# A maximum read ahead of the fifth gate of six, and a last output block emptied token by token

## The chip, the cores and the metric

The kernel runs on one core of one Trainium2 chip. The metric is the time of one launch on the device in microseconds (us), as the median of several runs. Five engines work side by side, each on its own queue of instructions in a fixed order: TensorE (PE, matmuls; PEld is its weight loads), VectorE (DVE), ScalarE (ACT), GpSimd (POOL) and SyncE (SP, which here only issues DMA transfers). They wait for each other by semaphores.

## The reference

Two stages, one behind the other: a convolution-like attention over the last seven positions with softmaxed weights, and a feed-forward layer with a sigmoid gate on its result.

```python
w = weight_gen - np.max(weight_gen, axis=-1, keepdims=True)     # weight_gen: (4, 4096, 8 heads, 7)
w = np.exp(w)
w = w / (np.sum(w, axis=-1, keepdims=True) + 1e-09)
x_pad = np.concatenate([np.zeros((B, pad, D), dtype=np.float32), x], axis=1)   # x: (4, 4096, 192)
x_unf = x_pad[:, idx, :].reshape(B, S, K, H, group)             # the 7 positions up to each one
x = np.einsum('bshk,bskhg->bshg', w, x_unf).reshape(B * S, D)   # 16384 tokens x 192
...
h = x @ w_in                                                    # 192 -> 2048
g = h * (1.0 / (1.0 + np.exp(-1.702 * h)))
return (g @ w_out).astype(np.float32)                           # 2048 -> 192
```

## The kernel before, in words

The 16384 tokens are cut into 32 **blocks** of 512 (4 tokens on each of 128 partitions), and the 2048 hidden features into 16 slices of 128. A **unit** is one slice for one block, 512 in all. Each unit goes through these steps:

- `whole` (L391 to L394): four matmuls of 512 columns write h into a PSUM bank, and `halves` (L403, L404) adds the small rest. The numbers are split into f16 parts so that the sums keep f32 quality.
- `gate`: ACT takes a tanh of the bank (L409, tile `th`), DVE multiplies it into the bank (L410).
- `split`: ACT writes the f16 high part (L415), DVE the low part (L416), both into the tile `g`.
- `second` (L426 to L428): twelve matmuls of 192 columns a unit add its share to the output banks `o`, two tokens to a bank.

Units are worked in **groups** of six (after a first short group of two), since six PSUM banks `h0` to `h5` hold h. Within a group PE runs three units' `whole`, all `halves`, and then, for the units 0 to 5 in turn, the seconds of the group before, mixed with the remaining three `whole`. `gate(u)` of a unit comes ahead of `split` of the unit before it in the order of DVE and ACT.

Beside this runs the preparation of later blocks, in **steps** that a table of numbers places: `plan([n - 7.4, ...], gen)` runs one step of a generator where the unit count reaches that number, and `until(end)` runs all steps that are due. `n` is the first unit of the group in which a block begins, so `n - 12` to `n - 6` is the group before the last one ahead of it. One generator, `scales(blk)`, finds the power of two by which a block is scaled. Its steps: DVE reduces the block to one value per partition (L234, L202, L207, tile `tf`); a one-column matmul on PE (L210) adds these up over the partitions into a PSUM bank (tile `top`); DVE reads it (**L216**); and three tiny DVE operations make the scale of it (`power`, L220 to L222). The bank that `top` borrows is `h2`, which the first unit of the next group needs: that unit's first matmul L391 may not start before L216 has read the bank. For block 1 it is an output bank `o` instead, which the next L426 needs.

The scaled block is then split (L275 on ACT, L278 on DVE, tile `xs`), turned by a DMA transpose (L284, tile `xt`), and half of it is copied by another DMA (L288, tile `xd`). L391 to L394 and L403 read `xt`, L404 reads `xd`.

At the start DVE and ACT also turn the raw weights into f16 parts (`parts_out`: L358 and L378 on ACT, L360 on DVE). `store` empties an output bank: ACT copies two tokens (L435) and SP stores the block (L440); the last block is stored in two halves.

Of the kernel before, what the change touches and what calls it, by code (L numbers as in the profile page):

```python
# [22 lines left out]
def conv_attention_then_ffn(  # L23
# [16 lines left out]
    J = 4  # L40
# [112 lines left out]
    def attend(blk):  # L153

        i, jb = divmod(blk, XB)
        w = wb[i][:, jb * J * H : (jb + 1) * J * H, :]
        xa[blk] = acc = apool.tile([P, J, D], F32, tag="acc", name="acc")
        for k in range(K):
            if k == 0:
                tap(blk, nc.gpsimd, acc, k, w)  # L160
            else:
                t = apool.tile([P, J, D], F32, tag="prod", name="prod", bufs=1)
                tap(blk, nc.gpsimd, t, k, w)
                nc.gpsimd.tensor_tensor(acc, acc, t, ALU.add)  # L164
            yield
# [261 lines left out]
        nc.tensor.matmul(o, lhsT=hi, rhs=wol[:, d], start=False, stop=False, skip_group_check=True)  # L427
        nc.tensor.matmul(o, lhsT=hi, rhs=woh[:, d], start=False, stop=z, skip_group_check=True)  # L428

    def store(blk, i, each=False):  # L430

        if i == 0:
            osb[blk] = opool.tile([P, J, D], F32, tag="osb", name="osb")
        j = slice(2 * i, 2 * i + 2)
        nc.scalar.activation(osb[blk][:, j, :], po.pop((blk, i)), AF.Copy, scale=scale[blk][:, 5:6])  # L435
        if i or each:
            j0 = 2 * i if each else 0
            b, t0 = blk // NJ, (blk % NJ) * J
            rows = out[b * S : (b + 1) * S, :].rearrange("(p t) d -> p t d", t=T)
            nc.sync.dma_start(rows[:, t0 + j0 : t0 + 2 * i + 2, :], osb[blk][:, j0 : 2 * i + 2, :])  # L440


    units = [(blk, f) for blk in range(NB) for f in range(NF)]
# [8 lines left out]
    def plan(slots, gen):  # L452
        for n in slots:
            todo.setdefault(math.floor(n), []).append((n, len(todo), gen))

    def once(fn, *args):
        fn(*args)
        yield
# [12 lines left out]
    def hold(t):  # L471

        nc.gpsimd.tensor_copy(held, t)

    with tc.manual_schedule():
        load_w(0)
        load_x(0, 0, J)
        load_tail(0)
        load_in(0)
        load_in(1)  # L480
        load_x(0, J, XB * J)
        load_in(2)
        load_tail(1)
        load_in(3)
        for c in range(4):
            load_out(c)
        load_w(1)
        load_x(1, 0, XB * J)
        constants()


        w_first = ps_h.tile([P, N], F32, tag="h0", name="w")[:, 0 : J * H * K].rearrange("p (n k) -> p n k", k=K)
        plan((-36.1, -35.7, -35.1, -34.6, -33.6), softmax(0, V, w_first))
        plan((-35.3, -34.7, -33.9, -33.2, -32.0), softmax(1, G_))
        plan((-36.2,), once(warm, 7, ident, P))
        plan((-32.1, -30.4, -27.7, -25.0), attend_first(w_first))
        plan((-24.9, -24, -23, -22, -21, -0.04, -0.03), attend(1))
        plan((-20.5, -18.3, -17.1, -17.1), scales(0))
        plan((-15.7, -13.6), split_first())
        raw = {"t": raw_t, "i": raw_i, "o": [raw_o[:, c * QC : (c + 1) * QC] for c in range(NO)]}  # L500
        for k, c, at, *slots in (
            ("t", 0, 0, -28.6, -23.2, -21.6),
            ("i", 0, 1, -27.4, -21.8, -19.7),
            ("i", 1, 2, -26.2, -18.4, -16.9),
            ("i", 2, 3, -24.6, -16.3, -14.5),
            ("t", 1, 4, -22.3, -14.9, -13.2),
            ("i", 3, 5, -20.4, -12.1, -10.1),
            ("o", 0, 6, -18.5, -10.7, -8.9),
            ("o", 1, 7, -13.9, -9.4, -7.5),
            ("o", 2, 8, -12.0, -7.2, -5.7),  # L510
            ("o", 3, 9, -10.8, -4.8, -0.6),
            ("o", 4, 10, -8.2, -0.05, 1.4),
            ("o", 5, 11, -6.3, 1.45, 1.9),
        ):
            plan(slots, narrow((k, c), raw[k][c], at))
        plan((-8.0, -7.1, -5.8), bound_in())
        plan((-5.0,), scales_gate(0))
        plan((-4.5, -3.5), parts_tail(0))
        plan((-3.8, -2.8), parts_in(0))
        plan((-0.05,), once(hold, w0l[:, DFF - 8 :]))  # L520
        plan((-2.75,), once(warm, 5, w0h, QC))
        plan((-3.2, -2.1), parts_in(1))
        plan((-2.5, -1.4), parts_tail(1))
        plan((-1.9, -0.7), parts_in(2))
        plan((-1.2, -0.06), parts_in(3))
        plan((1.95, 4.6, 4.65), bound_out())
        for c, slots in enumerate(((4.7, 5.2), (5.3, 5.8), (6.2, 6.7), (7.55, 7.9), (7.95, 8.1), (8.2, 8.6))):
            plan(slots, parts_out(c))
        plan((4.66,), scales_out(0))
        plan((7.7, 9.4, 9.45, 9.46), scales(1))  # L530
        plan((9.47,), scales_gate(1))
        plan((9.48,), scales_out(1))
        plan((9.49, 10.6), split_x(1))
        plan((10.65, 12), turn(1))

        for blk in range(2, NB):
            n = first(blk * NF)
            plan([n - 12.2, n - 7.4, n - 7.39, n - 7.38], scales(blk))
            plan([n - 6.28], scales_gate(blk))
            plan([n - 6.26], scales_out(blk))  # L540
            plan([n - 6.3, n - 6.2], split_x(blk))
            plan([n - 6.15, n - 5], turn(blk))
            if blk == 2:
                plan((-0.04, 0.5, 4.9, 6.4, 7.2, 7.25), softmax(blk, G_))
                plan((8.61,), once(lambda: hold(wos[:, NF * D - 8 :])))
                plan([8.62 + k for k in range(K)], attend(blk))
            elif blk == 3:
                plan((5.9, 7.26, 8.7, 10.7, 13.7, 17.6), softmax(blk, G_))
                plan([18 + 2 * k for k in range(K)], attend(blk))
            else:  # L550
                plan([n - 48.2, n - 48.1, n - 42.1, n - 36.15, n - 30.2, n - 30.1], softmax(blk, G_))
                plan([n - 30 + 2.2 * k for k in range(K)], attend(blk))
            if blk % XB == 0 and blk > XB:
                plan([blk * NF - 56.5], load_pair(blk // XB))

        def seconds(six):


            for z in zip(six[::2], six[1::2]):
                blk, f = z[0]  # L560
                for i in range(2):
                    if f in (0, NF - 2):
                        for j in (2 * i, 2 * i + 1):
                            for u in z:
                                second(u, j)
                        if f:
                            store(blk, i, each=blk == NB - 1)
                    else:
                        for j in range(J):
                            second(z[i], j)  # L570
                    yield

        sixes = [units[:few]] + [units[n : n + Q] for n in range(few, len(units), Q)]
        for k, us in enumerate([None] + sixes, -1):
            n, z = (min(todo), 0) if k < 0 else (units.index(us[0]), units.index(us[-1]) + 1)
            steps = sorted((t for i in range(n, z) for t in todo.get(i, ())), key=lambda t: t[:2])

            def until(end):
                while steps and steps[0][0] < end:
                    next(steps.pop(0)[2], None)  # L580

            if k < 0:
                until(z)
                continue
            due = seconds(sixes[k - 1] if k > 2 else sixes[0] + sixes[1] if k == 2 else ())
            early, late = us[:3], us[3:]
            if len(us) < Q:
                early, late = us, []
            for i, u in enumerate(early):
                bank(u)  # L590
                whole(u, True, False)
                if i == 1 or i == 0 and k > 2:
                    next(due, None)
                    until(n + 0.5 + 0.5 * i)
            for u in late:
                bank(u)
            for u, v in zip(us[::2], us[1::2]):
                halves(u, v, u in early, v in early)
            last = None
            for i, u in enumerate(us):  # L600
                if i > 1:
                    next(due, None)
                if u in late:
                    whole(u, False, True)
                gate(u)
                until(n + 0.5 + i)
                if last:
                    split(last)
                last = u
                until(min(n + 1 + i, z - 0.4))  # L610
            split(last)
            until(z)
            for _ in due:
                pass
        for _ in seconds(sixes[-1]):
            pass
# [29 lines left out]
```

## Time and profile before

| what | value |
|---|---|
| median of 3 runs | 1102.25 us (1102.07 to 1102.97) |
| the profiled execution's own time | 1101.69 us |
| its span, first to last instruction | 1099.7 us |
| mean granted clock of TensorE | 0.984 of full speed |
| busy: PE, DVE, ACT, POOL | 1050.0, 886.6, 703.6, 721.2 us |

The profile shows one execution. Its own time is 1.99 us longer than its span, which is what lies around the first and the last instruction; it is 0.56 us below the median of the three runs. An engine's busy time counts the whole of each matmul, though neighbours overlap; so PE's pace is read from the starts of its matmuls, not from their durations.

### The profile page before, as it was taken

Reading aid. Unit: us, or ns where it says so; the run is one execution under the profiler, and the core shown is the slowest. Engines: PE = TensorE matmul, PEld = TensorE weight load, DVE = VectorE, ACT = ScalarE, POOL = GpSimd, SP = SyncE. Lnnn points to the kernel's source line nnn. Section 1 sums busy time; section 2 is a strip of 40 time slices with the busy share of each in tenths; the row PEclk is TensorE's granted clock in tenths of the full one; section 3 lists DMA queues with packets and bytes.
Section 4 is the critical chain, followed back from the end, with each engine's and each line's share of the span. In section 5 each row is a group of like instructions: output and inputs, shape, how many; then the busy total and the mean of one; then the engine's idle time right before and its main releaser. Section 6 shows DMA issues by size and latency. Waiting matters only on the chain.

```text
span 1099.7 us, 22223 instructions
## 1 busy us (share of the span) xinstructions
PE 1050.0 (95%) x8821; PEld 732.6 (67%) x8821; DVE 886.6 (81%) x1556; ACT 703.6 (64%) x1251; POOL 721.2 (66%) x484
## 2 busy tenths in 40 slices
PE   4579999999999999999999999999999999999998
PEld 3146766676667676667766667666666766676666
DVE  8887877888797888879787877887887788788765
ACT  5765666666666666666666666656666666567655
POOL 4469758686855868685587768558775856786100
PEclk9689999999999999999999999999999999999999
DMA  9300120312012121301212120131212102101010
GB/s 305 119 17 16 39 83 18 91 32 91 15 32 77 32 91 32 87 18 32 76 33 90 32 80 27 32 77 32 88 35 74 33 17 91 33 21 44 15 30 18
DMA packets 73231, 60.71 MB, mean 55 GB/s; under 512 B 60588, under 2 KB 65964, under 8 KB 71592
## 3 DMA queue, kind: packets, MB, share of 16 engines
q1 hardware_dynamic: 73128, 59.30, 18.7%
q8 instruction: 69, 1.13, 0.4%
q14 instruction: 34, 0.28, 0.1%
HBM read 31.96 MB, written 12.58 MB: 41 GB/s over the span
## 4 chain that ended last, share of the span: by engine, by line
PE 83%; DVE 8%; ACT 6%; issue 2%; DMA 0%; ACTq 0%
PE o L426 14%; PE o L427 14%; PE o L428 14%; PE h L391 9%; PE h L392 9%; PE h L394 9%; PE h L393 9%; PE h L403 5%; DVE h L410 4%; ACT th L409 3%; DVE g L416 3%; ACT osb L435 1%; DVE tap L149 0%; ACT abs L337 0%; ACT g L415 0%
## 5 line engine op out<-in xcount | busy, mean ns | idle before, releaser
L426 PE MATMUL o<-wos,g 128*128 128x192 f16 x2048 | 505.7, 247 | 3.2 <-DVE s L216 3.2
L427 PE MATMUL o<-wol,g 128*128 128x192 f16 x2048 | 504.9, 247 | 0.5 <-DVE wol L360 0.5
L428 PE MATMUL o<-woh,g 128*128 128x192 f16 x2048 | 504.8, 246 | 0.0
L410 DVE SCALAR_TENSOR_TENSOR h<-th,h 128x512 f32<-128x512 f32 x512 | 347.0, 693 | 181.7 <-ACT th L409 174.6
L409 ACT ACTIVATE th<-h,s 128x512 f32<-128x512 f32 x512 | 342.4, 686 | 231.8 <-PE h L404 135.8
L416 DVE SCALAR_TENSOR_TENSOR g<-g,h 128x512 f16<-128x512 f16 x512 | 349.2, 682 | 13.7 <-ACT g L415 2.0
L164 POOL TENSOR_TENSOR acc<-acc,prod 128x768 f32<-128x768 f32 x186 | 346.3, 1862 | 14.6
L415 ACT ACTIVATE g<-h 128x512 f16<-128x512 f32 x512 | 305.0, 596 | 44.1 <-DVE h L410 44.1
L149 POOL TENSOR_TENSOR prod<-xb,wb 128x768 f32<-128x768 f32 x186 | 288.9, 1553 | 11.1
L426 PEld LDWEIGHTS <-g 128*128 128x128 f16 x2048 | 200.4, 98 | 75.7 <-issue 35.9
L427 PEld LDWEIGHTS <-g 128*128 128x128 f16 x2048 | 200.6, 98 | 39.5 <-issue 3.2
L391 PE MATMUL h<-xt,w0l 128*128 128x512 f16 x512 | 195.1, 381 | 10.4 <-DVE s L216 10.4
L428 PEld LDWEIGHTS <-g 128*128 128x128 f16 x2048 | 200.7, 98 | 0.8 <-issue 0.7
L394 PE MATMUL h<-xt,wth 128*128 128x512 f16 x512 | 195.1, 381 | 0.0
L393 PE MATMUL h<-xt,w0h 128*128 128x512 f16 x512 | 195.1, 381 | 0.0
L392 PE MATMUL h<-xt,w0h 128*128 128x512 f16 x512 | 195.1, 381 | 0.0
L143 POOL TENSOR_TENSOR wb<-wb,wr 128x224 f32<-128x224 f32 x31 | 17.9, 576 | 229.1 <-DVE wr L140 225.6
L278 DVE SCALAR_TENSOR_TENSOR xs<-acc,s,xs 128x512 f16<-128x512 f32 (+1 forms) x62 | 102.3, 1689 | 0.0
L394 PEld LDWEIGHTS <-wth 128*128 128x128 f16 x512 | 50.3, 98 | 61.1 <-issue 1.1
L393 PEld LDWEIGHTS <-w0h 128*128 128x128 f16 x512 | 50.2, 98 | 61.1 <-issue 1.1
L403 PE MATMUL h<-xt,tl 64*128 64x512 f16 x256 | 70.6, 381 | 2.4 <-DVE g L416 2.4
L404 PE MATMUL h<-xd,tl 64*128 64x512 f16 x256 | 70.7, 381 | 2.0 <-DVE g L416 2.0
(92 smaller groups left out, 523.2 us busy)
## 6 DMA issues: line engine op xcount, KB each, us to landing
xb<-in_x_dram SPq DMA_DIRECT2D x12, 1344.0 KB, 6.4
out_dram<-osb SPq DMA_DIRECT2D x31, 384.0 KB, 2.4
wb<-in_weight_gen_dram SPq DMA_DIRECT2D x16, 224.0 KB, 3.2
ro<-in_moe_w_out_dram SPq DMA_DIRECT2D x4, 768.0 KB, 12.3
xb<-in_x_dram SPq DMA_DIRECT2D x3, 768.0 KB, 7.4
ri<-in_moe_w_in_dram SPq DMA_DIRECT2D x4, 512.0 KB, 8.6
xb<-in_x_dram SPq DMA_DIRECT2D x4, 504.0 KB, 5.2
xd<-xt SPq DMA_DIRECT2D x31, 64.0 KB, 2.1
```

The lines of the kernel that those rows point to most:

```text
L164: nc.gpsimd.tensor_tensor(acc, acc, t, ALU.add)
L391: nc.tensor.matmul(ps, lhsT=w0l[:, s], rhs=x0, start=start, stop=False)
L392: nc.tensor.matmul(ps, lhsT=w0h[:, s], rhs=x2, start=False, stop=False)
L393: nc.tensor.matmul(ps, lhsT=w0h[:, s], rhs=x0, start=False, stop=False)
L394: nc.tensor.matmul(ps, lhsT=th_[:, s], rhs=x1, start=False, stop=stop)
L409: nc.scalar.activation(t, hp[u], AF.Tanh, scale=scale[u[0]][:, 4:5])
L410: nc.vector.scalar_tensor_tensor(hp[u], t, 1.0, hp[u], ALU.add, ALU.mult)
L415: nc.scalar.activation(g[:, 0], hp[u], AF.Copy, scale=2.0**-12)
L416: nc.vector.scalar_tensor_tensor(g[:, 1], g[:, 0], -(2.0**12), hp.pop(u), ALU.mult, ALU.add)
L426: nc.tensor.matmul(o, lhsT=lo, rhs=wos[:, d], start=a and j % 2 == 0, stop=False, skip_group_check=True)
L427: nc.tensor.matmul(o, lhsT=hi, rhs=wol[:, d], start=False, stop=False, skip_group_check=True)
L428: nc.tensor.matmul(o, lhsT=hi, rhs=woh[:, d], start=False, stop=z, skip_group_check=True)
```

## The change

It has three parts. First, a new call `until(n + 0.25 + i)` ahead of `gate(u)`: steps whose number lies less than 0.25 past a unit now come ahead of that unit's gate instead of behind it. Second, the table: for the blocks 2 to 31 the matmul of the maximum and its read L216 move from 4.6 to 4.1 units into their group, ahead of the gate of the fifth unit, and `power` stays near where it was. For block 1 the same two move ahead of the third unit's `whole`, and some of the weight parts move behind them. Third, `store` for the last block: ACT copies the first token of each pair and stores it from its own queue, DVE copies the second token, and SP stores that.

```diff
-    def store(blk, i, each=False):
+    def store(blk, i, last=False):
...
+        b, t0 = blk // NJ, (blk % NJ) * J
+        rows = out[b * S : (b + 1) * S, :].rearrange("(p t) d -> p t d", t=T)
+        o, s = po.pop((blk, i)), scale[blk][:, 5:6]
+        if last:
+            j = 2 * i
+            nc.scalar.activation(osb[blk][:, j, :], o[:, 0, :], AF.Copy, scale=s)
+            nc.scalar.dma_start(rows[:, t0 + j, :], osb[blk][:, j, :])
+            nc.vector.tensor_scalar(osb[blk][:, j + 1, :], o[:, 1, :], s, None, ALU.mult)
+            nc.sync.dma_start(rows[:, t0 + j + 1, :], osb[blk][:, j + 1, :])
+            return
+        nc.scalar.activation(osb[blk][:, 2 * i : 2 * i + 2, :], o, AF.Copy, scale=s)
+        if i:
+            nc.sync.dma_start(rows[:, t0 : t0 + J, :], osb[blk])
...
-        for c, slots in enumerate(((4.7, 5.2), (5.3, 5.8), (6.2, 6.7), (7.55, 7.9), (7.95, 8.1), (8.2, 8.6))):
+        for c, slots in enumerate(((4.7, 5.2), (5.3, 5.8), (6.2, 6.7), (7.55, 7.9), (7.95, 8.92), (8.2, 8.96))):
...
-        plan((7.7, 9.4, 9.45, 9.46), scales(1))
+        plan((7.7, 8.9, 8.91, 9.46), scales(1))
...
-            plan([n - 12.2, n - 7.4, n - 7.39, n - 7.38], scales(blk))
+            plan([n - 12.2, n - 7.9, n - 7.89, n - 7.3], scales(blk))
...
-                plan((8.61,), once(lambda: hold(wos[:, NF * D - 8 :])))
-                plan([8.62 + k for k in range(K)], attend(blk))
+                plan((8.97,), once(lambda: hold(wos[:, NF * D - 8 :])))
+                plan([8.98 + k for k in range(K)], attend(blk))
...
-                            store(blk, i, each=blk == NB - 1)
+                            store(blk, i, last=blk == NB - 1)
...
+                until(n + 0.25 + i)
                 gate(u)
```

What stands where, at three places. The first is DVE's queue in the group in which block 2 is scaled; the same piece comes back for each of the blocks 2 to 31. The numbers behind the names count buffers and differ between the two programs only because the order does.

```order
 L410 SCALAR_TENSOR_TENSOR h_993<-th_1050,h_993 128x512
 L416 SCALAR_TENSOR_TENSOR g_1053<-g_1053,h_988 128x512
-L410 SCALAR_TENSOR_TENSOR h_994<-th_1072,h_994 128x512
-L416 SCALAR_TENSOR_TENSOR g_1078<-g_1078,h_993 128x512
-L216 TENSOR_SCALAR s_939<-top_1081 128x1
+L216 TENSOR_SCALAR s_939<-top_1075 128x1
+L410 SCALAR_TENSOR_TENSOR h_994<-th_1078,h_994 128x512
+L416 SCALAR_TENSOR_TENSOR g_1081<-g_1081,h_993 128x512
 L220 TENSOR_SCALAR s_939<-s_939 128x1
 L221 TENSOR_SCALAR s_939<-s_939 128x1
```

L216 has moved past one gate (L410, of the fifth unit) and one split (L416, of the fourth). On PE the matmul L210 of these blocks stands where it stood.

The second place is PE's queue at the start, in the group of units 8 to 13. Before, ahead of the first L426 of that group's later seconds (the rows above these are the third unit's `whole` and the other `halves`):

```order
L403 LDWEIGHTS tl
L403 MATMUL h<-xt,tl 128x512
L404 LDWEIGHTS tl
L404 MATMUL h<-xd,tl 128x512
L210 LDWEIGHTS ones
L210 MATMUL top<-tf,ones 128x1
L426 LDWEIGHTS g
L426 MATMUL o<-wos,g 128x192
```

And now, behind the twelve seconds that stand between the second and the third unit:

```order
L428 LDWEIGHTS g
L428 MATMUL o<-woh,g 128x192
L210 LDWEIGHTS ones
L210 MATMUL top<-tf,ones 128x1
L391 LDWEIGHTS w0l
L391 MATMUL h<-xt,w0l 128x512
L392 LDWEIGHTS w0h
L392 MATMUL h<-xt,w0h 128x512
```

Block 1's L210 has moved ahead of the third unit's `whole` (four matmuls) and all six `halves`, which now stand behind it.

The third place is the end of the program, on DVE and then on ACT, with the semaphores that each instruction waits for (PE_49, DVE_49 and Activation_49 are raised by the engine of that name, DMAHW ones by transfers). DVE now:

```order
L410 SCALAR_TENSOR_TENSOR h<-th,h 128x512 [waits DVE_49,Activation_49]
L416 SCALAR_TENSOR_TENSOR g<-g,h 128x512 [waits Activation_49] x2
L442 TENSOR_SCALAR osb<-o,s 128x192 [waits DMAHW6_49,DMAHW0_49,Activation_49]
L442 TENSOR_SCALAR osb<-o,s 128x192 [waits Activation_49]
L649 UNCONDITIONAL_BRANCH
```

ACT now:

```order
L415 ACTIVATE g<-h 128x512 [waits DVE_49] x2
L440 ACTIVATE osb<-o,s 128x192 [waits DMAHW6_49,PE_49]
L441 DMA out_dram<-osb 128x192 [waits DMAHW2_49,Activation_49]
L440 ACTIVATE osb<-o,s 128x192 [waits PE_49]
L441 DMA out_dram<-osb 128x192 [waits DMAHW4_49,Activation_49]
```

Where ACT had two copies of 128x384 and SP two stores, ACT has two copies of 128x192 and two stores, DVE has two copies, and SP two stores. DVE's copies wait for ACT and not for PE.

## Rows read from the trace of the kernel before

**Rows 1.** The page, part 1: busy us of each engine (share of span), instructions.

```profile
PE 1050.0 (95%) x8821; PEld 732.6 (67%) x8821; DVE 886.6 (81%) x1556; ACT 703.6 (64%) x1251; POOL 721.2 (66%) x484
```

**Rows 2.** PE's waits from 100 to 1090 us: total us, times, longest.

```profile
PE h L391 <- DVE s L216: 10.4, 30, 0.3
```

**Rows 3.** Windows: us, busy of PE, PEld, DVE, ACT, POOL, clock, DMA share, GB/s.

```profile
500.00:1000.00 500.00, 494.82 (x4210) 346.29 (x4209) 408.37 (x710) 321.37 (x571) 349.24 (x229) 1.00 0.18 50
```

**Rows 4.** Timeline of PE: start us, us, engine, line, tiles, [idle before <-releaser].

```profile
505.75 0.38 PE L394 MATMUL h<-xt,wth 128*128 128x512 f16 x1
505.96 0.38 PE L391 MATMUL h<-xt,w0l 128*128 128x512 f16 x1
...
517.75 0.38 PE L394 MATMUL h<-xt,wth 128*128 128x512 f16 x1
518.47 0.38 PE L391 MATMUL h<-xt,w0l 128*128 128x512 f16 x1 [0.34 <-DVE s L216]
...
530.45 0.38 PE L391 MATMUL h<-xt,w0l 128*128 128x512 f16 x1
```

**Rows 5.** Timeline of all engines around one read of the maximum.

```profile
515.82 0.68 DVE L416 SCALAR_TENSOR_TENSOR g<-g,h 128x512 f16<-128x512 f16 x1
...
516.09 0.17 PE L210 MATMUL top<-tf,ones 128*128 128x1 bf16 x1
...
517.07 0.70 DVE L410 SCALAR_TENSOR_TENSOR h<-th,h 128x512 f32<-128x512 f32 x1 [0.57 <-ACT th L409]
...
518.27 0.15 DVE L216 TENSOR_SCALAR s<-top 128x1 int32<-128x1 int32 x1
```

**Rows 6.** Timeline of PE at the start, block 1's maximum.

```profile
58.76 0.38 PE L394 MATMUL h<-xt,wth 128*128 128x512 f16 x1
...
65.45 0.16 PE L210 MATMUL top<-tf,ones 128*128 128x1 bf16 x1 [0.72 <-DVE tf L207]
68.77 0.32 PE L426 MATMUL o<-wos,g 128*128 128x192 f16 x1 [3.15 <-DVE s L216]
...
71.60 0.36 PE L426 MATMUL o<-wos,g 128*128 128x192 f16 x1
...
72.23 0.38 PE L391 MATMUL h<-xt,w0l 128*128 128x512 f16 x1
```

**Rows 7.** Timeline of DVE at the start.

```profile
65.31 2.06 DVE L360 SCALAR_TENSOR_TENSOR wol<-ro,sc,woh 128x512 f16<-128x512 f32 x3
...
68.56 0.15 DVE L216 TENSOR_SCALAR s<-top 128x1 int32<-128x1 int32 x1
```

**Rows 8.** A window at the start; the granted clock is third from the end.

```profile
62.00:64.00 2.00, 0.52 (x1) 0.10 (x1) 2.00 (x6) 2.00 (x5) 0.97 (x2) 0.50 0.00 0
```

**Rows 9.** Timeline: issues of the copies xd, and the first matmul that reads block 1's.

```profile
80.12 0.62 SPq L288 DMA_DIRECT2D xd<-xt  x1
...
84.67 0.38 PE L404 MATMUL h<-xd,tl 64*128 64x512 f16 x1
...
504.56 0.62 SPq L288 DMA_DIRECT2D xd<-xt  x1
```

**Rows 10.** DMA issues: KB each, median us from issue to landing.

```profile
xd<-xt SPq DMA_DIRECT2D x31, 64.0 KB, 2.1
xt<-xs SPq DMA_TRANSPOSE x31, 3.7
out_dram<-osb SPq DMA_DIRECT2D x2, 192.0 KB, 1.9
```

**Rows 11.** Timeline of the last microseconds.

```profile
1095.78 1.32 SPq L440 DMA_DIRECT2D out_dram<-osb  x2
...
1096.17 0.58 ACT L435 ACTIVATE osb<-o,s 128x384 f32<-128x384 f32 x1 [0.41 <-PE o L428]
```

**Rows 12.** Groups by line and form: busy us, mean ns of one, idle before.

```profile
L134 DVE TENSOR_REDUCE wm<-wb 128x32 f32<-128x224 f32 x32 | 12.0, 374 | 0.2 <-ACT wb L132 0.2
L132 ACT ACTIVATE wb<-wb 128x224 f32<-128x224 f32 x32 | 12.2, 380 | 0.5 <-POOL wb L130 0.5
```

More of the change, by code (lines that the diff above doesn't have):

```diff
@@ L428, in second @@
         nc.tensor.matmul(o, lhsT=hi, rhs=woh[:, d], start=False, stop=z, skip_group_check=True)
-    def store(blk, i, each=False):
+    def store(blk, i, last=False):
         if i == 0:
             osb[blk] = opool.tile([P, J, D], F32, tag="osb", name="osb")
[L434 to L440, printed above, removed]
+        b, t0 = blk // NJ, (blk % NJ) * J
[11 more added lines that the diff above has]
+            nc.sync.dma_start(rows[:, t0 : t0 + J, :], osb[blk])
     units = [(blk, f) for blk in range(NB) for f in range(NF)]
```

## Prediction

> **What bounds the kernel now.** I read the page's busy shares first [rows 1]: PE is busy 95% of the span, no other engine above 81%. That says which engine to look at, and not whether it ever stands still. So the second view is the list of PE's waits between 100 and 1090 us [rows 2]. It has one row: thirty times L391 waits for L216, 10.4 us in all. Thirty is the number of the blocks 2 to 31. In the 500 us from 500 to 1000, PE's idle time is 5.2 us at a granted clock of 1.00 [rows 3]; with some fifteen of these waits there, at 0.35 us each, that is all of it. So in steady state PE is the bound, and this wait is the only thing that ever holds it.
>
> Idle time understates what it costs, because matmuls overlap. The third view is PE's timeline [rows 4]. Where nothing waits, the next group's first L391 starts 0.21 us behind the L394 ahead of it (505.75 to 505.96). Where it waits, it starts 0.72 us behind (517.75 to 518.47). The loss is 0.51 us, not the 0.34 us printed as idle: the difference is the overlap that was lost too. The length of whole groups agrees: 12.51 us from 505.96 to 518.47, with the maximum in it, and 11.98 us from 518.47 to 530.45, without. The difference of 0.53 us is the wait and about 0.02 us for L210.
>
> **Why L391 waits, and what the move does.** The maximum is on PE at 516.09 us and ends 0.17 us later, at 516.26 [rows 5]. DVE finishes the split of the third unit (L416, 515.82 and 0.68 long) at 516.50, and is then idle for 0.57 us until the tanh of the fifth unit comes at 517.07. Before the change L216 stands behind that gate and the next split, so it starts at 518.27, although its data have been there for 2 us; PE wanted the bank at 517.75 + 0.21 = 517.96. With the change L216 is the next instruction behind the split that ends at 516.50. Its 0.15 us, or 0.19 us from start to start, fits in the hole of 0.57 us, and the bank is free near 516.7, 1.3 us before PE asks for it. The fifth gate behind it on DVE is still released by its tanh. Where another block's group has no such hole, the gate would start up to 0.19 us later, and the scale operations behind it 0.19 us earlier, since L216 no longer stands there.
>
> So the price is 30 times 0.51 us = **15.3 us**. The lower end is the idle column alone, 10.4 us. I take 15.3, since starts of matmuls set the pace, and the group lengths say the same.
>
> What is late next? The first unit's bank also needs its own split, five units earlier, so nothing else of DVE's is near. The `xt` of the next block is nearer. For the blocks whose first unit opens a group (every third), the transpose has landed at 504.56, when SP goes on to its `xd` copy, and L391 reads it at 505.96 [rows 4, 9]: a slack of 1.4 us. PE comes 0.5 us earlier, the transpose 0.1 to 0.2 us (L278 stands behind the scale operations), so 1.0 us is left.
>
> **The start.** Here the change adds a wait. Block 1's L210 now stands ahead of the third unit's `whole`, which ran to 58.76 + 0.38 us before [rows 6]. Its input `tf` is not ready before 65.45, so PE's queue, `whole` and all `halves`, is held up behind it from about 58 us. I move 65.45 to 65.7, for the weight parts and reciprocal that now go ahead of gates delay the gates, and with them the reduction, by about a quarter microsecond. What is given back: L216 stood behind three L360 and two gates, and ran at 68.56; PE's L426 waited 3.15 us for it [rows 6, 7]. Now it stands behind one L360, near 66.3, while PE works off what was held up.
>
> How long that takes depends on the clock. The granted clock was 0.50 from 62 to 64 us, after PE had worked only in pieces since 59 [rows 8]; after 68.77 its matmuls of 192 columns started every 0.157 us (18 from 68.77 to 71.60), and at 72.23 it is back at the 0.38 us of a full-speed L391 [rows 4, 6]. At the low level, `whole` takes 4 times 0.42 us and the paired `halves` 3 times 0.42 us (twice the 0.21 us from one matmul of 512 columns to the next [rows 4]), 2.9 us. PE would reach L426 at 65.7 + 2.9 = 68.6, hardly before the 68.77 of now. If the clock comes back as long after PE resumes as it did (3.1 us from 68.77), the 19 matmuls that ran at 0.157 us run at half that, and 1.5 us are gained. If it comes back no earlier than it did, nothing is. A further bound: block 1's `xd`, issued at 80.12 and landing 2.1 us later at 82.2, is read at 84.67 [rows 9, 10]; its chain goes through the gates behind the `halves` and would be about 1.2 us later, at 83.4, so PE can use some 1.2 us of a gain and no more. Bounds 0 and 1.5 us; I take **1.0 us**, nearer the clock that returns.
>
> **The end.** Before, ACT's copy starts 0.04 us behind the last matmul, takes 0.58 us, and SP's second store is issued at 1095.78 + 1.32 - 0.33 = 1096.77 us [rows 11]. Now two engines share the bank, but not at once: in the order above, DVE's copy waits for ACT's semaphore and for none of PE's, so the ACT copy must itself wait for the bank's last matmul, and the two stand one behind the other. A copy of 192 columns lies near the rows of 224: 0.38 us on ACT, 0.37 us on DVE [rows 12], a little less for fewer columns. 0.36 + 0.03 + 0.35 = 0.74 us in place of 0.58: +0.16 us. The transfer shrinks from 192 KB to 96; rows near it land in 1.9 us (192 KB) and 2.1 us (`xd`, 64 KB) [rows 10], so I count no gain and bound it by 0.3 us. ACT's own store is issued 0.35 us ahead of SP's; that it is the first from that queue has no row here, and I bound it by the slowest median landing of that list, 3.7 us, less 1.9 and 0.35: up to +1.4 us. I take **+0.2 us**, bounds -0.3 and +1.6.
>
> On emptying a bank by two engines, the Trainium skill (PSUM — Partial Sum Buffer, section "PSUM bank collisions raise a hardware error") says that ScalarE and VectorE may not touch one bank's partitions at the same time, reads included. By that the copies cannot overlap, as the waits say; if they did overlap, this term would be 0.36 - 0.58 = -0.2 us in place of +0.2. On the two queues, the skill (DMA: Bandwidth & Descriptors, "Issuing engines are not separate DMA queues") says that transfers from either run on the same engines, and only the time of issuing is saved; no run here shows it yet, and by it the store could gain at most one issue of 0.33 us.
>
> **The sum**, against the profiled execution: 1101.69 - 15.3 - 1.0 + 0.2 = 1085.6 us. The median lies 0.56 us above that execution, so I predict **1086.0 us** for the median.
>
> **Rivals.**
> - *It comes back as a wait for `xt`.* If PE, 0.5 us faster a block, meets late transposes in the ten blocks that open a group, each gives its 0.5 us back: 5 us, 1091 us. For it: the transposes share the DMA engines with loads and stores. Against it: the slack is 1.4 us and [rows 2] shows not one wait of PE for a transfer.
> - *Only the printed idle time is won*, because the overlap of the matmuls has to be built up again anyway: 10.4 us, 1091 us. Against it are the 0.21 us without a wait [rows 4].
> - *L216 doesn't move in time.* It now waits for PE on DVE's queue. If `top` came later than 517.07, the fifth gate and all behind it would be late. At 1.3 us late the bank is late as well and the old wait is back, near 1101 us. The trace has `top` 0.8 us before that gate, so this has little for it.
> - *Slower*: the start. PE stands for some 7 us in one piece in place of three shorter ones. If the granted clock then stays low, PE does half its work. This decides from about 30 us at the low level (15.3 us lost) and gives 1103 us or more. Against it: the level came back within 3.1 us of steady work after 68.77, when PE had also been idle for 3 us at once.
>
> **Chances and range.** The forecast 0.80, with its own range from 1084.2 (start 1.5, end -0.3) to 1087.8 us (start 0, end +1.2). The first two rivals together 0.14, the third 0.03, the slower one 0.03. The range for 8 in 10 reaches from 1084.2 to 1091 us, as the second group lies at its upper edge. About 0.2% is what a measurement of this kernel can tell from no change: 2.2 us. Faster 0.95, same 0.02, slower 0.03.
>
> **What would show it.** Right: PE's waits from 100 to 1090 us no longer name L216, nor a transfer in its place; groups with a maximum last 12.0 us; L216 starts right behind L210, ahead of L410. At the start a long wait of L210 for `tf` of about 7 us and the first L391 of the second half (72.23 before) near 71. At the end ACT's copy, then DVE's, not side by side. Wrong: a new row of 0.3 us or more, thirty or ten times, in PE's waits; or a granted clock of 0.5 beyond 72 us.

## The result, and the profile after

| | before | after |
|---|---|---|
| median | 1102.53 us (1102.07 to 1102.97, 4 runs) | **1085.45 us** (1085.03 to 1085.65, 4 runs) |
| profiled execution: its time, its span | 1101.69, 1099.7 us | 1085.65, 1083.8 us |
| mean granted clock | 0.984 | 0.984 |

The ratio is 0.9845, with a 95% interval of 0.9828 to 0.9862: 17.1 us less. The forecast was 1086.0 us, with a range of 1084.2 to 1091.0.

I read the same views as before the change, in the same order. First part 1 of the page (busy us of each engine, its share of the span, instructions), as in [rows 1]:

```profile
PE 1045.7 (96%) x8821; PEld 733.8 (68%) x8821; DVE 877.2 (81%) x1558; ACT 702.7 (65%) x1251; POOL 722.9 (67%) x484
```

The same 8821 matmuls, in 16 us less. Next PE's waits from 40 us to the last store (total us, times, longest), to be set beside [rows 2]:

```profile
PE top L210 <- DVE tf L207: 8.3, 1, 8.3
PE h L403 <- DVE g L416: 0.8, 1, 0.8
PE top L210 <- DVE tf L205: 0.6, 1, 0.6
PE h L404 <- DVE g L416: 0.2, 1, 0.2
```

The thirty waits for L216 are gone, and nothing stands in their place; all four rows lie ahead of 66 us, and from 100 us on the view has no row at all. The window that answers to [rows 3] says the same (us, busy of PE, PEld, DVE, ACT, POOL, clock, DMA share, GB/s):

```profile
500.00:1000.00 500.00, 500.00 (x4276) 351.55 (x4274) 410.41 (x722) 325.75 (x579) 363.66 (x236) 1.00 0.18 51
```

PE is busy in 500.00 of 500 us, and 4276 matmuls fit there where 4210 did. One read of the maximum, in the timeline of PE and DVE (start us, us, engine, line, tiles, [idle before <-releaser]), beside [rows 4, 5]:

```profile
498.68 0.38 PE L391 MATMUL h<-xt,w0l 128*128 128x512 f16 x1
...
508.54 0.68 DVE L416 SCALAR_TENSOR_TENSOR g<-g,h 128x512 f16<-128x512 f16 x1
508.81 0.17 PE L210 MATMUL top<-tf,ones 128*128 128x1 bf16 x1
509.14 0.15 DVE L216 TENSOR_SCALAR s<-top 128x1 int32<-128x1 int32 x1
509.79 0.70 DVE L410 SCALAR_TENSOR_TENSOR h<-th,h 128x512 f32<-128x512 f32 x1 [0.50 <-ACT th L409]
510.47 0.38 PE L394 MATMUL h<-xt,wth 128*128 128x512 f16 x1
510.68 0.38 PE L391 MATMUL h<-xt,w0l 128*128 128x512 f16 x1
...
522.66 0.38 PE L391 MATMUL h<-xt,w0l 128*128 128x512 f16 x1
```

L216 follows the split, and the bank is read at 509.14 + 0.15 = 509.29, 1.39 us before PE's L391 at 510.68 (the prediction said 1.3). That L391 starts 0.21 us behind the L394 ahead of it, not 0.72. The fifth gate is still released by its tanh, so L216 sits in a hole. The group with the maximum lasts 510.68 - 498.68 = 12.00 us, the one behind it 11.98.

The start, PE and DVE, beside [rows 6, 7]:

```profile
53.83 0.21 DVE L353 TENSOR_SCALAR sc<-sc 128x1 f32<-128x1 f32 x1
...
65.13 0.19 DVE L207 TENSOR_REDUCE tf<-ta 128x1 bf16<-128x32 f32 x1
65.37 0.16 PE L210 MATMUL top<-tf,ones 128*128 128x1 bf16 x1 [8.31 <-DVE tf L207]
65.89 0.15 DVE L216 TENSOR_SCALAR s<-top 128x1 int32<-128x1 int32 x1
...
68.60 0.34 PE L426 MATMUL o<-wos,g 128*128 128x192 f16 x1
...
71.52 0.38 PE L391 MATMUL h<-xt,w0l 128*128 128x512 f16 x1
73.37 0.38 PE L391 MATMUL h<-xt,w0l 128*128 128x512 f16 x1
```

PE now stands once, for 8.31 us, and the wait of L426 for L216 is gone. But L426 comes at 68.60 in place of 68.77: what PE had put off until then, it does at half speed. The windows show how long (granted clock third from the end):

```profile
58.00:60.00 2.00, 0.00 (x0) 0.00 (x0) 1.57 (x4) 0.95 (x4) 0.00 (x0) 1.00 0.00 0
60.00:62.00 2.00, 0.00 (x0) 0.00 (x0) 1.56 (x4) 2.00 (x5) 0.00 (x0) 0.58 0.00 0
...
69.00:70.00 1.00, 1.00 (x8) 0.95 (x7) 0.96 (x4) 0.11 (x1) 1.00 (x1) 0.50 0.00 0
70.00:71.00 1.00, 1.00 (x11) 0.96 (x10) 0.59 (x4) 0.86 (x2) 0.92 (x2) 0.72 0.00 0
```

The clock is at its upper level (2.4 GHz) until about 60 us, then at the lower (1.2 GHz), and back within the window from 70 to 71: some 5 us after PE resumed at 65.37. The first L391 of the second half stands at 71.52, where [rows 6] have 72.23.

The end, timeline of PE, ACT and DVE, and the two rows of the list of transfers (KB each, median us to landing), beside [rows 10, 11]:

```profile
1079.99 0.25 PE L428 MATMUL o<-woh,g 128*128 128x192 f16 x1
...
1080.28 0.42 ACT L440 ACTIVATE osb<-o,s 128x192 f32<-128x192 f32 x1 [0.57 <-PE o L428]
1080.73 0.42 DVE L442 TENSOR_SCALAR osb<-o,s 128x192 f32<-128x192 f32 x1 [0.57 <-ACT osb L440]
...
out_dram<-osb ACTq DMA_DIRECT2D x2, 96.0 KB, 1.7
out_dram<-osb SPq DMA_DIRECT2D x2, 96.0 KB, 1.6
```

The two copies stand one behind the other, 0.87 us in all in place of 0.58, and each half store lands 0.2 to 0.3 us sooner than the whole one.

Between the first L391 of the second half and the last L428 lie 1079.99 - 71.52 = 1008.47 us, before the change 1095.88 - 72.23 = 1023.65. So of the 15.9 us between the spans 15.2 are the steady part, 0.7 the start, and the end is nothing (from the last matmul's start to the span's end 3.81 us, before 3.82). The rows of the kernel before that this rests on, beside [rows 6]:

```profile
54.27 0.21 DVE L353 TENSOR_SCALAR sc<-sc 128x1 f32<-128x1 f32 x1
...
1095.88 0.25 PE L428 MATMUL o<-woh,g 128*128 128x192 f16 x1
```

The first of them says that the 0.7 us is not all the change's. L353 stands ahead of everything that was moved, and it ran at 54.27 us before and at 53.83 after: 0.44 us of the 0.7 were there already. Between these two executions the new start itself gave 0.3 us.

### The profile page after: what moved, and what is told of

It is laid out like the page before. It is cut to its first block, busy times and chain, and to the rows that moved or that the text cites. A ratio compares the mean times of both kernels' runs of the same rounds, so it can differ in the third digit from the quotient of the medians.

```text
span 1083.8 us, 22229 instructions
## 1 busy us (share of the span) xinstructions
PE 1045.7 (96%) x8821; PEld 733.8 (68%) x8821; DVE 877.2 (81%) x1558; ACT 702.7 (65%) x1251; POOL 722.9 (67%) x484
## 4 chain that ended last, share of the span: by engine, by line
PE 94%; DVE 3%; ACT 2%; issue 1%; ACTq 0%
PE o L426 16%; PE o L428 16%; PE o L427 16%; PE h L392 10%; PE h L391 10%; PE h L394 10%; PE h L393 10%; PE h L403 6%; DVE tap L149 1%; ACT abs L337 0%; ACT bits L326 0%; DVE g L416 0%; DVE h L410 0%; DVE m L332 0%; ACT m L329 0%
## 5 line engine op out<-in xcount | busy, mean ns | idle before, releaser
L426 PE MATMUL o<-wos,g 128*128 128x192 f16 x2048 | 505.0, 247 | 0.0
L428 PE MATMUL o<-woh,g 128*128 128x192 f16 x2048 | 504.2, 246 | 0.0
L410 DVE SCALAR_TENSOR_TENSOR h<-th,h 128x512 f32<-128x512 f32 x512 | 347.0, 693 | 177.1 <-ACT th L409 169.6
L416 DVE SCALAR_TENSOR_TENSOR g<-g,h 128x512 f16<-128x512 f16 x512 | 349.2, 682 | 14.0 <-ACT g L415 2.2
L426 PEld LDWEIGHTS <-g 128*128 128x128 f16 x2048 | 200.3, 98 | 75.8 <-issue 36.1
L428 PEld LDWEIGHTS <-g 128*128 128x128 f16 x2048 | 200.6, 98 | 0.0
L391 PE MATMUL h<-xt,w0l 128*128 128x512 f16 x512 | 195.3, 381 | 0.0
L394 PE MATMUL h<-xt,wth 128*128 128x512 f16 x512 | 195.1, 381 | 0.0
L278 DVE SCALAR_TENSOR_TENSOR xs<-acc,s,xs 128x512 f16<-128x512 f32 (+1 forms) x62 | 94.7, 1566 | 0.0
L394 PEld LDWEIGHTS <-wth 128*128 128x128 f16 x512 | 50.3, 98 | 61.1 <-issue 1.3
```

What stands on the lines that cost most here:

```text
L391: nc.tensor.matmul(ps, lhsT=w0l[:, s], rhs=x0, start=start, stop=False)
L394: nc.tensor.matmul(ps, lhsT=th_[:, s], rhs=x1, start=False, stop=stop)
L410: nc.vector.scalar_tensor_tensor(hp[u], t, 1.0, hp[u], ALU.add, ALU.mult)
L416: nc.vector.scalar_tensor_tensor(g[:, 1], g[:, 0], -(2.0**12), hp.pop(u), ALU.mult, ALU.add)
L426: nc.tensor.matmul(o, lhsT=lo, rhs=wos[:, d], start=a and j % 2 == 0, stop=False, skip_group_check=True)
```

## The experiments

The theory: the bank is the cause. PE loses, from start to start, all the time by which L216 is late for the bank, the start gives about 1 us, the end nothing. Rivals: only the printed idle time comes back; or it is L216's new place on DVE that helps; or the gain belongs to the start or the end. The first four kernels ran together, with a median of 1101.91 us for the kernel before (1101.17 to 1103.41, 21 runs).

**The steady part alone.** Onto the kernel before:

```diff
-            plan([n - 12.2, n - 7.4, n - 7.39, n - 7.38], scales(blk))
+            plan([n - 12.2, n - 7.9, n - 7.89, n - 7.3], scales(blk))
...
+                until(n + 0.25 + i)
                 gate(u)
```

> The read of the maximum moved for the blocks 2 to 31 alone (with the new call ahead of the gate); block 1's steps and the last block's stores as before. If each of the 30 waits costs its lost start-to-start time of 0.51 us: 15.3 us less than the kernel before, some 1087.2 us. If each costs only the printed idle time of 0.35 us: 10.4 us less, some 1092 us, and the start and the end of the whole change would have to give the other 6.6 us. In the profile PE has no wait for L216 from 100 to 1090 us in either case, but block 1's wait of about 3.2 us at the start stays.

Measured: 1086.95 us (1086.69 to 1088.14), ratio 0.9867 (0.9852 to 0.9882). That is 15.0 us less (13.0 to 16.3 by the interval), 0.50 us for each of the thirty waits; the rival of the printed idle time, 10.4 us, is out. In the trace PE has no wait for L216 from 100 us on, and block 1's wait of 3.2 us stays, both as expected.

**The start alone.** Onto the kernel before, the call of `until` as above and

```diff
-        for c, slots in enumerate(((4.7, 5.2), (5.3, 5.8), (6.2, 6.7), (7.55, 7.9), (7.95, 8.1), (8.2, 8.6))):
+        for c, slots in enumerate(((4.7, 5.2), (5.3, 5.8), (6.2, 6.7), (7.55, 7.9), (7.95, 8.92), (8.2, 8.96))):
...
-        plan((7.7, 9.4, 9.45, 9.46), scales(1))
+        plan((7.7, 8.9, 8.91, 9.46), scales(1))
...
-                plan((8.61,), once(lambda: hold(wos[:, NF * D - 8 :])))
-                plan([8.62 + k for k in range(K)], attend(blk))
+                plan((8.97,), once(lambda: hold(wos[:, NF * D - 8 :])))
+                plan([8.98 + k for k in range(K)], attend(blk))
```

> Block 1's part alone (its maximum ahead of the third unit, the weight parts behind it, with the new call); the table of the blocks 2 to 31 and the end as before. If the start is worth what the two profiles show between 58 and 72 us less what one was already ahead at 54 us: 0.3 us less than before, 1102.2 us. If it is worth the predicted term: 1.0 us less. If the printed idle time were the price of the 30 waits, the start and the end together would have to be worth 6.6 us. PE's wait for L216 in steady state stays at about 10.4 us in 30 times.

Measured: 1100.32 us (1099.92 to 1101.84, 11 runs), ratio 0.9988 (0.9979 to 0.9997): 1.6 us less by the medians, 0.3 to 2.3 by the interval. PE's waits from 54 us on show both the new wait and the old thirty. Since this kernel has the new call too, and the thirty waits stay, it was the moved numbers of the table and not the call by itself that gave the 15.0 us above.

```profile
PE h L391 <- DVE s L216: 10.4, 30, 0.3
PE top L210 <- DVE tf L207: 8.3, 1, 8.3
```

**The end alone.** The kernel before with the new `store` and its call, as in the diff of the change.

> The end alone: the last block emptied by ACT and then DVE, a token each, stored by two queues; all else as before. By the profiles (3.82 us from the last matmul's start to the end of the span before, 3.81 after) no change, 1102.5 us within 0.4 us. By the predicted term 0.2 us more. If two engines and two queues were worth something by themselves: up to 1 us less. DVE's copy waits for ACT's in every case.

Measured: 1102.3 us (1101.61 to 1103.34, 11 runs), ratio 1.0002 (0.9994 to 1.0011): 0.4 us more by the medians, from 0.7 less to 1.2 more by the interval. Two engines and two queues for the last block are worth nothing that can be measured, in either direction.

**Another bank, the old place.** L216 stays where it was; for the blocks 2 to 31 `top` borrows the second unit's bank in place of the first unit's:

```diff
-        yield from top_of(t, e, False, ("h3", "o")[blk] if blk < 2 else "h2")
+        yield from top_of(t, e, False, ("h3", "o")[blk] if blk < 2 else "h3")
```

> The kernel before with one name changed: the maximum of the blocks 2 to 31 borrows the bank of the group's second unit (h3) in place of the first's (h2), which is wanted some 1.9 us later; L216 stays behind the fifth gate. If the bank is what PE waits for: no wait for L216 in steady state, and 15.3 us less than before, some 1087.2 us, the same as the moved read. If the place of L216 on DVE's queue matters by itself (its delay of the gates, or the scale operations behind it), this kernel stays above the moved read by that much: most of the 15 us would stay.

Measured: 1087.1 us (1086.56 to 1087.69), ratio 0.9866 (0.9853 to 0.988), 14.8 us less: the whole gain of the steady part, with L216 as late on DVE as ever. Timeline of PE and DVE:

```profile
510.59 0.17 PE L210 MATMUL top<-tf,ones 128*128 128x1 bf16 x1
...
512.47 0.38 PE L391 MATMUL h<-xt,w0l 128*128 128x512 f16 x1
512.77 0.15 DVE L216 TENSOR_SCALAR s<-top 128x1 int32<-128x1 int32 x1
```

The group's first L391 starts at 512.47, 0.30 us ahead of L216, since it no longer needs what L216 reads. So it is the bank, and not the place on DVE.

**L216 later still.** If lateness is lost one for one, more of it must cost in proportion. Onto the kernel before, L216 goes behind the gate of the sixth unit:

```diff
-            plan([n - 12.2, n - 7.4, n - 7.39, n - 7.38], scales(blk))
+            plan([n - 12.2, n - 7.4, n - 6.9, n - 6.89], scales(blk))
```

> The kernel before, with L216 of blocks 2 to 31 one unit later on DVE, behind the gate of the sixth unit and the split of the fifth. Theory (the whole delay of the bank is PE's loss, from start to start): L216 moves from 518.27 to about 519.55 in the group read, PE's loss per block grows from 0.51 to 1.8 us, 30 times 1.28 us is 38 us, and the time is 1138 to 1142 us. Rival (part of the loss is given back by the gates and banks that PE's later start makes wait less): well under 1130.

Measured: 1141.56 us (1139.92 to 1141.61), ratio 1.0348 (1.0334 to 1.0363), beside a median of 1102.34 us for the kernel before: 39.2 us more. PE's waits from 100 us on, and one of them in the timeline:

```profile
PE h L391 <- DVE s L216: 48.8, 30, 1.6
...
510.05 0.38 PE L394 MATMUL h<-xt,wth 128*128 128x512 f16 x1
...
511.85 0.15 DVE L216 TENSOR_SCALAR s<-top 128x1 int32<-128x1 int32 x1
...
512.06 0.38 PE L391 MATMUL h<-xt,w0l 128*128 128x512 f16 x1 [1.63 <-DVE s L216]
```

From L394 to L391 it is now 2.01 us: 1.80 lost, against 0.51 before the move, and 30 x 1.29 = 38.7 us. The printed idle time is too low by 0.17 us in both kernels (0.34 for 0.51, 1.63 for 1.80). That constant is the overlap of two matmuls (0.38 us long, 0.21 us from start to start): a small share of a long wait and a third of a short one.

**The reduction earlier.** After the change PE's one long wait is L210 for `tf`. Block 1's reduction (L234, L202, L207) stands on DVE behind weight parts that are not needed sooner. Onto the kernel after:

```diff
-        plan((7.7, 8.9, 8.91, 9.46), scales(1))
+        plan((4.68, 8.9, 8.91, 9.46), scales(1))
```

> The changed kernel, with block 1's reduction (L234, L202, L207) worked ahead of the weight parts of the third slice on DVE in place of behind them; PE's order is the changed kernel's. Theory (what is left of the start is the 8.3 us for which L210 waits for tf): tf is ready some 9 us earlier, the third unit's whole and the halves run at 56 to 62 us, PE comes to the next L426 near 66 in place of 68.6, and the time is 2 to 3 us under the changed kernel's 1085.5, so 1082.5 to 1083.5. Rival (the granted clock, or the gates that the reduction now delays on DVE, take it back): 1085 to 1087.

Measured: 1083.65 us (1082.91 to 1085.44), ratio to the kernel before 0.9832 (0.9818 to 0.9846). Its range touches that of the kernel after, and the two had not run together, so both ran once more, side by side.

> The changed kernel itself, once more, on the same chip as the kernel with the early reduction, so that the two can be compared. Both theories: 1085 to 1086.

Measured: 1085.77 us (1085.3 to 1086.11, 4 runs), ratio to the kernel before 0.9851 (0.9838 to 0.9865).

> The kernel with the early reduction of block 1 once more, beside the changed kernel. If the 1.8 us between their medians are the start's: 1.4 to 2.6 us below the changed kernel of this call (the profile shows 2.4 us between the second units of that group). If they are a difference of chips: within 0.5 us of it.

Measured: 1083.77 us (1083.15 to 1084.14, 5 runs), ratio to the kernel before 0.9832 (0.9819 to 0.9845). The ranges of the two lie apart, and the medians by 2.0 us: this version beats the kernel after as well, by the low end of the 2 to 3 us that were expected of it. PE's timeline, from its first run, shows where it gains and where it gives back:

```profile
56.79 0.17 PE L210 MATMUL top<-tf,ones 128*128 128x1 bf16 x1
...
60.73 0.39 PE L404 MATMUL h<-xd,tl 64*128 64x512 f16 x1 [1.93 <-DVE g L416]
62.82 0.39 PE L403 MATMUL h<-xt,tl 64*128 64x512 f16 x1 [1.71 <-DVE g L416]
...
64.32 0.32 PE L426 MATMUL o<-wos,g 128*128 128x192 f16 x1
...
68.11 0.63 PE L391 MATMUL h<-xt,w0l 128*128 128x512 f16 x1
...
70.95 0.38 PE L391 MATMUL h<-xt,w0l 128*128 128x512 f16 x1
```

L210 does not wait, and L426 comes 4.3 us before the 68.60 of the kernel after. From there PE works at the low level for all 24 matmuls of L426 to L428 and the next four of 512 columns (0.63 us each); at 70.95 it is 2.4 us ahead of the 73.37, of which 0.45 us were there already at L353 (53.38 and 53.83). So of 4.3 us about 2.0 are left. The windows of that run:

```profile
60.00:62.00 2.00, 0.39 (x1) 0.09 (x1) 2.00 (x4) 2.00 (x4) 0.26 (x1) 1.00 0.00 0
62.00:64.00 2.00, 0.79 (x2) 0.19 (x2) 1.92 (x4) 1.95 (x5) 0.85 (x2) 0.82 0.00 0
...
70.00:71.00 1.00, 1.00 (x14) 1.00 (x12) 1.00 (x3) 0.60 (x2) 1.00 (x1) 0.95 0.00 0
```

The clock falls some 3 us later than in the kernel after, and is back at about the same time. The rival (the clock takes it back) is right in part: from L426 on PE spends 5.8 us at the low level (64.32 to 70.10) and loses half of that, 2.9 us; in the kernel after it is 2.0 us (68.60 to 70.56) and 1.0.

## Why the prediction was right

- **The steady part, 30 x 0.51 = 15.3 us.** Right: 15.2 us in the profiles, 15.0 with the steady part alone, 14.8 by way of another bank. That starts of matmuls set the pace, and not the idle column, is shown from two sides, by what came back and by what the later read cost.
- **The hole on DVE.** Right in each step: L216 behind the split, the bank free 1.39 us ahead, the fifth gate released by its tanh, 12.00 us a group.
- **The start, 1.0 us between 0 and 1.5.** The mechanism was right (L426 hardly earlier, the gain hanging on the clock); its size lies between 0.3 us in the two profiles and 1.6 in the medians of the start alone. That L426 came at 68.60, just as worked out (68.6), is luck. L210 came at 65.37 and not at 65.7, since this execution was 0.44 us ahead, and `whole` and `halves` took 3.23 us from L210 on, not 2.9. Counted from L353, L426 came 0.27 us later than before. The wait of L210 was 8.31 us where I had written about 7. The profiles show why the size depends on what one compares. The table takes DVE's L353 and from it the time to the L391 after the one at 72.23 in [rows 6]; these are starts in the timelines. The last column is worked out from the granted clock of windows of 1 and 2 us, as those above.

| order at the start | L353, that L391 | between | clock low |
|---|---|---|---|
| old, kernel before | 54.27, 74.09 | 19.82 us | 61.6 to 71.9 us |
| old, later read | 55.83, 75.48 | 19.65 | 66.2 to 73.1 |
| old but for the new call, steady part alone | 53.43, 74.64 | 21.21 | 63.2 to 73.5 |
| old, end alone | 54.44, 75.70 | 21.26 | 64.7 to 75.0 |
| old, other bank | 54.04, 75.16 | 21.12 | 64.0 to 74.3 |
| new, kernel after, twice | 53.83, 73.37 and 54.06, 73.68 | 19.54, 19.62 | 60.3 to 70.6, 60.7 to 71.0 |
| new, start alone | 53.89, 73.43 | 19.54 | 60.4 to 70.6 |
| new with early reduction, twice | 53.38, 70.95 and 54.01, 71.50 | 17.57, 17.49 | 63.3 to 70.1, 63.7 to 70.6 |

With the old order that L391 came early in two of five profiles and some 1.4 us later in three. The two are early for different reasons: in the kernel before the clock fell only 7.4 us behind L353 and was low for 10.2 us; in the later read it fell 10.4 us behind L353 and was low for 6.8 us; in the three others it fell 9.8 to 10.3 us behind L353 and was low for 10.2 us. The execution from which the term was sized was one of the early ones. Against the two early ones the new order gains 0.1 to 0.3 us, against the others 1.6. Also, the lower bound of the term rested on "no earlier than it did", and the upper on "as long after PE resumes as it did"; in the kernel after it was about 5 us behind PE's start, between the two.
- **The end, +0.2 us.** The copies are one behind the other, as the waits said, and take 0.42 us each, not 0.36 and 0.35: 0.87 us for 0.58, +0.29 us. The transfer's 0.2 to 0.3 us, kept as a bound, pays for that. Sum 0.0, and the end alone shows no change either. ACT's first store cost nothing visible: the bound of +1.4 us on an unused queue was too wide. The Trainium skill (DMA: Bandwidth & Descriptors, "Issuing engines are not separate DMA queues") says that a second issuing engine gives no engines of its own; the traces agree as far as they go, with 1.7 us on ACT's queue and 1.6 on SP's, and no gain in the time. Which engines carried the stores no row here shows.
- **The sum and its range.** The range of the forecast was added up wrongly. By its own terms, from the 1102.25 us of the median, it reaches from 1102.25 - 15.3 - 1.5 - 0.3 = 1085.15 us to 1102.25 - 15.3 + 1.2 = 1088.15, and not from 1084.2 to 1087.8; its upper end also took 1.2 us for the end of the program, where the bound worked out above it was 1.6. The measured 1085.45 us lies in either range. Between the two profiles the sum came out almost to the digit (1085.6 forecast, 1085.65 measured), and that is in part luck: the start gave 0.7 us less than its term, and what made up for most of it was that the end cost 0.2 us less and that the later execution was 0.44 us ahead at L353, which no term foresaw.
- **The rivals.** No wait for `xt` came up. In the timelines of SP and PE, from the `xd` copy, to which SP goes on when the transpose has landed, to the L391 that reads it, the ten blocks that open a group had 1.03 to 3.00 us before and have 0.55 to 2.51 us now. In eight of the ten the slack shrank by about half a microsecond or more, and five of them are at 0.96 to 1.04 us, where I had reckoned with 1.0; in the block of [rows 9] it grew, from 1.40 us to 2.24 (496.44 to 498.68). The printed idle time alone is refuted by the steady part alone. L216 did move in time. The start did not turn slower: the clock was at its lower level for some 10 us, not 30.

What stays open: what decides, in the old order, when the clock falls, and whether it is then low for 10.2 us or for 6.8. The time of L353 alone doesn't tell the three late profiles from the two early ones (53.43 to 54.44 against 54.27 and 55.83). The new order was alike in its three profiles; that it always is, three do not show.

## What to carry to other kernels

A short wait of PE between overlapped matmuls costs more than its printed idle time: measure from start to start in a place with the wait and in one without, and multiply by the count. When a tiny read holds a bank, there are two cures of equal worth, reading it earlier or borrowing a bank that is wanted later, and the second was one word here. At a start with a low clock, time won ahead of the low stretch comes back only in part, so size such a term from several executions and not from one.

## What the runs showed of the hardware that I had not expected

A copy of 128x192 f32 from PSUM took 0.42 us on ACT and on DVE alike, more than the 0.37 to 0.38 us of 224 columns in [rows 12]: the count of columns alone did not give the one from the other. And PE standing still for 8.31 us kept the low level until about 5 us after it resumed (60.3 to 70.6 us), while PE working in pieces through the same stretch (early reduction) kept the upper level some 3 us longer, and yet had it back within the same window, 70 to 71 us: the low stretch was 6.8 us long there, against 10.2 us.
